# A sigmoid bias as a constant, and the last score visit of the first pass ahead of all value products

## The chip, the cores and the metric

One core of a Trainium2 chip runs the whole kernel. TensorE (PE in the profile, its weight loads PEld) multiplies, VectorE (DVE) copies, adds and transposes blocks of 32 x 32, ScalarE (ACT) applies the sigmoids, GpSimd (POOL) issues all loads, and SyncE (SP) issues the stores. The metric is the device time of one execution in microseconds; the number given for a kernel is the median of its runs.

## The reference

```python
def _attn_ref(q, k, v):                       # 8 batches, 12 heads, 448 positions, head size 64
    scores = scale * np.matmul(q, k.transpose(0, 1, 3, 2)) - np.log(S)     # scale = 1/8
    attn = 1.0 / (1.0 + np.exp(-scores))
    return np.matmul(attn, v)

def _moe_ref(x, w_in, w_out, beta):           # x: 3584 x 768, w_in: 768 x 2048, w_out: 2048 x 768
    h = x @ w_in
    g = h * (1.0 / (1.0 + np.exp(-beta * h)))
    return g @ w_out
```

The attention has a sigmoid in place of a softmax, with the constant -log(448) added to every scaled score. Its result, heads side by side, is x of the two dense layers; between them every hidden column has its own `beta`. All inputs and the output are float32.

## The kernel before

**Tiling.** Loads turn everything into float16. A batch has 448 positions, which are three full key tiles of 128 and a last one of 64 (`JF` = 3, `KL` = 64). Heads are taken four at a time as a *group* `g` (three groups for each batch, `QPB`), and two at a time as a *slot* `s` (a group has slots 2g and 2g+1). The four heads of a group lie in the four blocks of 32 partitions, so q and k are made ready by DVE's 32 x 32 transposes (`transpose`, L174), and four score matmuls of 32 contraction rows run beside each other.

**Scores and values.** A score tile is two PSUM banks. PE writes scores into it (`score`, L198), ACT turns it into weights by one sigmoid over 128 x 896 (`weigh`, L210, its instruction is L212), and `attend` (L256) multiplies the weights with v into a PSUM bank, from where DVE copies them to `xT` (L276). The last key tile has only 64 rows, so the two slots of a group share one score tile for it, one in the upper and one in the lower 64 partitions. For that, the 64 rows of v must be there twice: `double_v_last` (L141) copies them from partitions 0 to 63 to 64 to 127 on DVE. An even slot reads the rows as loaded, an odd slot the copied ones (`last_base`).

**Dense layers.** `dense1` (L281) makes one of 16 column tiles of the hidden layer: six matmuls with w_in, a sigmoid on ACT with scale `beta` (L293) and a product on DVE (L296). The second layer is written out as `dense2` (L307) for some row tiles and as a seven-product scheme (`strassen`, L388) for pairs of the others. Their units are a stream of *filler* (`filler_stream`, L467) that is put between the score visits, so that PE has work while ACT computes.

**The opening.** The order of every queue is that of the program: nothing reorders the list. The first batch is special. Its queries are done in two halves of 224 columns (`QH`). `half_visit(g, c0, second)` (L238) computes key tiles 0 and 1 of a group, or with `second` tiles 2 and 3, always into two score tiles; the second of the two in a `second` visit is only half full (448 columns of sigmoid). In the first pass (c0 = 0) there are six such visits, in the loop at L525. Here six PSUM banks are three score tiles, used in turn, one bank holds the idle matmuls and one more is free for values (`share_psum(firsts, 3, 2)`); later there are two score tiles and four other banks. Between the visits, `idle_units` (L507) multiplies a tile of zeros; the visits and these units are all the work PE has until v is there. Before the change, right after the fifth visit, slot 0's values (`attend(0, 0, QH, (0,))`) are issued, then the doubling of v's last rows, then the transposition of the second half of q of group 0, then two idle units, and only then the sixth visit. After the loop come slot 1's values, the first visit of the second pass, and the values of slots 2 to 5.

**The loads.** POOL issues in this order: q (first half) and k of group 0, the two memsets of L498 and L499, q and k of groups 1 and 2, four pieces of v and two pieces with v's last 64 rows, the second halves of q of groups 0 to 2, then w_in in eight pieces of 256 hidden columns (`load_w_in`, L147), of which each serves two `dense1` units. Then come the next groups and w_out. A load waits on POOL until the load eight places before it has landed, since they share a semaphore.

The constant of the sigmoid is in `nlogs`, a column of 128 x 1 that POOL fills at L498, and L212 takes it as `bias=nlogs[:, 0:1]`.

Of the kernel before, what the change touches and what calls it, by code (L numbers as in the profile page):

```python
# [8 lines left out]
FP32 = mybir.dt.float32  # L9
# [4 lines left out]
def kernel(  # L14
# [10 lines left out]
    nc = tc.nc  # L25
# [6 lines left out]
    P = 128  # L32
    BLK = 32
    HQ = P // BLK
    NB = S // BLK
# [5 lines left out]
    QPB = H // HQ  # L41
# [5 lines left out]
    QH = S // 2  # L47
    MSCALE = 1.0 / math.sqrt(D)
    NEG_LOG_S = -math.log(float(S))
# [3 lines left out]
    const = ctx.enter_context(tc.tile_pool(name="const", bufs=1))  # L53
# [30 lines left out]
    def bank(name: str, cols: int = S, hold=None):  # L84
        i = min((i for i in used if i not in held.values()), key=used.get)
        touch(i)
        if hold is not None:
            held[hold] = i
        return psum["one"].tile([P, cols], FP32, tag=f"one{i}", name=name)


    nlogs = const.tile([P, 1], FP32, name="nlogs")
    dummy = const.tile([P, 1], FP32, name="dummy")
    beta_in = const.tile([BLK, P], FP32, name="beta_in")
    beta_sb = const.tile([P, BLK], FP32, name="beta_sb")
# [11 lines left out]
    def load_one(g: int, r: int, c0: int = 0, c1: int = NB):  # L107
        b, t = divmod(g, QPB)
        if g not in raws:
            raws[g] = rawp.tile([P, 2, NB, D], FP16, tag="raw", name="raw")  # L110
        nc.gpsimd.dma_start(  # L111
            out=raws[g][:, r, c0:c1].rearrange("p c d -> p (c d)"),
            in_=(q, k)[r][b, HQ * t : HQ * (t + 1)].rearrange("h (p c) d -> (h p) (c d)", c=NB)[
                :, c0 * D : c1 * D
            ],
        )
# [8 lines left out]
    def last_base(s: int) -> int:  # L125
        return (s % 2 ^ swapped(s // 2)) * KL
# [14 lines left out]
    def double_v_last(b: int):  # L141
        nc.vector.tensor_copy(out=vs[b][KL:P, :, JF], in_=vs[b][0:KL, :, JF])
# [27 lines left out]
    def in_order(b: int, t):  # L170
        t = t.rearrange("p c e -> p (c e)").bitcast(FP32)
        return t.rearrange("p (q c) -> p c q", c=NB) if b == B - 1 else t

    def transpose(g: int, r: int, c0: int = 0, c1: int = NB):  # L174
        raw = raws[g][:, r]
        if r == 0:
            if g not in qT:
                qT[g] = qTp.tile([P, NB * BLK, PAIR], FP16, tag="qT", name="qT")
            nc.vector.transpose(  # L179
                out=in_order(g // QPB, qT[g][:, c0 * BLK : c1 * BLK]),  # L180
                in_=raw[:, c0:c1].rearrange("p c d -> p (c d)").bitcast(FP32),
            )
            return
        kT[g] = kTp.tile([P, S, PAIR], FP16, tag="kT", name="kT")
        to = kT[g].rearrange("p k e -> p (k e)").bitcast(FP32)
        frm = raw.rearrange("p c d -> p (c d)").bitcast(FP32).rearrange("p (c f) -> p c f", c=NB)
        nc.vector.transpose(
            out=to[:, 0 : JF * P].rearrange("p (j i q) -> p i j q", j=JF, i=HQ),
            in_=frm[:, 0:NF].rearrange("p (i j) f -> p i j f", j=JF),
        )  # L190
        nc.vector.transpose(  # L191
            out=to[:, JF * P :], in_=frm[:, NF:].rearrange("p c f -> p (c f)")
        )
# [16 lines left out]
    def weigh(sco, n: int):  # L210
        at = attnp.tile([P, 2, S], FP16, tag="attnT", name="attnT")
        nc.scalar.activation(  # L212
            out=at[:, :, 0:n],
            in_=sco[:, :, 0:n],
            func=AF.Sigmoid,
            bias=nlogs[:, 0:1],
            scale=MSCALE,
        )
        return at


    def visit(g: int, jt: int, also=()):
        if jt < JF:
            todo = [(score_tile(), [s]) for s in (2 * g, 2 * g + 1)]
        else:
            todo = [(score_tile(), [2 * h, 2 * h + 1]) for h in (g, *also)]
        for e in range(PAIR):
            for sco, slots in todo:
                for s in slots:
                    for hh in range(2):  # L230
                        score(sco, 0, s, jt, hh, e, 0, S)
        for sco, slots in todo:
            at = weigh(sco, S)
            for s in slots:
                at_tiles[s, jt, 0] = at


    def half_visit(g: int, c0: int, second: int):  # L238
        slots = (2 * g, 2 * g + 1)
        scos = [score_tile() for _ in slots]  # L240
        plan = [(s, jt, sco, jt * QH) for jt in (0, 1) for s, sco in zip(slots, scos)]
        widths = [S, S]
        if second:
            plan = [(s, 2, sco, 0) for s, sco in zip(slots, scos)]
            plan += [(s, JF, scos[0], QH) for s in slots]
            widths = [S, QH]
        for i in range(0, len(plan), 2):
            for e in range(PAIR):
                for s, jt, sco, u0 in plan[i : i + 2]:
                    for hh in range(2):  # L250
                        score(sco, u0, s, jt, hh, e, c0, QH)
        ats = {id(sco): weigh(sco, n) for sco, n in zip(scos, widths)}
        for s, jt, sco, u0 in plan:
            at_tiles[s, jt, c0] = ats[id(sco)][:, :, u0 : u0 + QH]

    def attend(g: int, c0: int, n: int, part=(0, 1)):  # L256
        b, t = divmod(g, QPB)
        if b not in xTs:
            xTs[b] = xTp.tile([P, NHC, S], FP16, tag="xT", name="xT")
        slots = [2 * g + x for x in part]  # L260
        avs = [bank("av_ps") for _ in slots]
        todo = [(s, av, jt) for s, av in zip(slots, avs) for jt in range(JF)]
        for s, av, jt in todo + [(s, av, JF) for s, av in zip(slots, avs)]:
            at = at_tiles.pop((s, jt, c0))
            base, nk = (last_base(s), KL) if jt == JF else (0, P)
            for hh in range(2):
                nc.tensor.matmul(  # L267
                    av[hh * D : (hh + 1) * D, 0:n],
                    vs[b][base : base + nk, 2 * (s % NPAIR) + hh, jt],
                    at[base : base + nk, hh, 0:n],  # L270
                    start=(jt == 0),
                    stop=(jt == JF),
                    tile_position=(base, hh * D),
                )
        for s, av in zip(slots, avs):
            nc.vector.tensor_copy(out=xTs[b][:, s % NPAIR, c0 : c0 + n], in_=av[:, 0:n])  # L276
# [215 lines left out]
    NH = NB // 2  # L492
    firsts = ctx.enter_context(ExitStack())
    share_psum(firsts, 3, 2)
    with tc.manual_schedule():
        load_one(0, 0, 0, NH)
        load_one(0, 1)
        nc.gpsimd.memset(nlogs, NEG_LOG_S)  # L498
        nc.gpsimd.memset(dummy, 0.0)  # L499
        nc.scalar.activation(out=dummy, in_=dummy, func=AF.Sigmoid, bias=0.0, scale=1.0)  # L500

# [5 lines left out]
        def idle_units(n: int):  # L507
            for _ in range(n):
                nc.tensor.matmul(idle, still[:, 0:P], still, start=True, stop=True)  # L509
# [15 lines left out]
        for g in range(QPB):  # L525
            for second in range(2):
                half_visit(g, 0, second)
                if (g, second) == (QPB - 1, 0):
                    attend(0, 0, QH, (0,))
                    double_v_last(0)  # L530
                    transpose(0, 0, NH, NB)
                if 2 * g + second < 2 * QPB - 1:
                    idle_units(4 if g < QPB - 1 else 2)
        attend(0, 0, QH, (1,))
        half_visit(0, QH, 0)
        attend(1, 0, QH, (0,))
# [121 lines left out]
```

## Time and profile before

| what | value |
|---|---|
| timed runs | 388.84, 389.12 and 390.28 us, median 389.12 us |
| the profiled execution | span 388.2 us, by the page its whole time; the median is 0.9 us above it |
| PE / ACT / DVE / POOL busy | 381.5 / 241.5 / 229.7 / 67.3 us |
| score sigmoids (L212) | 171, of which 165 over 128 x 896 (1004 ns each) and 6 over 128 x 448 (627 ns each) |
| granted TensorE clock | 1.000 |
| loads and stores | 34.30 MB, mean 88 GB/s; 190 to 204 GB/s from 19 to 68 us |

A busy share is an average: a kernel whose PE is busy for 98% of the span is bound by PE nearly everywhere, and what else can be gained lies in the few places in which PE stands. The mean of one instruction is its latency, from start to written result; where two follow each other without a gap, the second starts before the first has ended, and the distance of the starts is the shorter number that counts for throughput. The busy spans of matmuls overlap in the same way, so a wait shorter than about a quarter of a microsecond does not show as idle time.

### The profile page before, as it was taken

How to read it: one execution, taken by the hardware profiler on the slowest of the kernel's cores; microseconds unless marked ns; L12 is line 12 of the kernel's file. 1: busy time of each engine (PE TensorE's matmuls, PEld its weight loads, DVE VectorE, ACT ScalarE, POOL GpSimd, SP SyncE). 2: the span in 40 equal slices, each digit the busy share in tenths (PEclk: the TensorE clock that was granted, in tenths of full speed). 3: DMA queues.
4: the chain of work that ended last, by engine and by line, in shares of the span. 5: the costliest groups of instructions: out<-in, count | busy, mean ns of one | idle time of the engine just before them, and what ended most of it. 6: DMA issues, size and time to landing. Idle time of an engine off the chain costs nothing.

```text
span 388.2 us, 7376 instructions
## 1 busy us (share of the span) xinstructions
PE 381.5 (98%) x2991; PEld 191.4 (49%) x2991; DVE 229.7 (59%) x437; ACT 241.5 (62%) x329; POOL 67.3 (17%) x117
## 2 busy tenths in 40 slices
PE   8899999999999999999999999999999999999996
PEld 3477754444545444444554445544445444555563
DVE  2356463885766556655765656664676565655762
ACT  4887865687565796497365783568853677625200
POOL 7833343122110410140110410104100000000000
PEclk9999999999999999999999999999999999999999
DMA  7999999629243760446353561629113300030033
GB/s 112 172 191 203 198 204 199 144 55 112 47 91 70 126 80 14 105 79 66 49 115 74 87 71 34 127 60 144 28 21 83 82 2 2 0 83 0 2 81 122
DMA packets 42401, 34.30 MB, mean 88 GB/s; under 512 B 21872, under 2 KB 38784, under 8 KB 42368
## 3 DMA queue, kind: packets, MB, share of 16 engines
q0 software_dynamic: 36976, 22.81, 42.8%
q1 hardware_dynamic: 5392, 11.02, 11.0%
q8 instruction: 23, 0.38, 0.4%
q14 instruction: 10, 0.08, 0.1%
HBM read 45.62 MB, written 11.01 MB: 146 GB/s over the span
## 4 chain that ended last, share of the span: by engine, by line
PE 93%; DMA 3%; ACT 2%; POOL 0%; issue 0%; DVE 0%; POOLq 0%
PE m_ps L285 39%; PE m_ps L397 29%; PE sco L201 11%; PE av_ps L267 10%; PE m_ps L315 4%; ACT attnT L212 2%; DMA raw<-in_k_dram 2%; DMA v<-in_v_dram 1%; POOL raw L111 0%; PE idle_ps L509 0%; ACT sg L293 0%; DVE osb L328 0%; DVE gt L296 0%; POOL nlogs L498 0%; POOL dummy L499 0%
## 5 line engine op out<-in xcount | busy, mean ns | idle before, releaser
L212 ACT ACTIVATE attnT<-sco,nlogs 128x896 f16<-128x896 f32 (+1 forms) x171 | 160.3, 991 | 84.3 <-PE sco L201 83.5
L285 PE MATMUL m_ps<-xT,w_in 128*128 128x448 f16 (+1 forms) x864 | 154.7, 332 | 0.4 <-DVE gt L296 0.3
L296 DVE TENSOR_TENSOR gt<-m_ps,sg 128x448 f16<-128x448 f32 (+1 forms) x144 | 79.8, 572 | 84.4 <-ACT sg L293 84.3
L285 PEld LDWEIGHTS <-w_in 128*128 128x128 f16 x864 | 80.6, 98 | 70.9 <-issue 15.5
L293 ACT ACTIVATE sg<-m_ps,beta_sb 128x448 f32<-128x448 f32 (+1 forms) x144 | 81.8, 595 | 31.3 <-PE m_ps L285 30.1
L397 PEld LDWEIGHTS <-sum 128*128 128x128 f16 x480 | 45.2, 98 | 36.4 <-issue 7.9
L201 PE MATMUL sco<-qT,kT 32*128 32x448 f16 (+3 forms) x864 | 52.6, 340 | 1.3 <-ACT attnT L212 1.1
L397 PE MATMUL m_ps<-w_T,sum 128*128 128x384 f16 x288 | 51.6, 327 | 0.0
L111 POOL DMA_DIRECT2D raw<-in_q_dram x27 | 14.8, 550 | 189.7 <-DVE kT L191 183.1
L416 DVE TENSOR_TENSOR osb<-m_ps,osb 128x384 f32<-128x384 f32 x60 | 33.3, 555 | 18.7 <-PE m_ps L397 16.9
L267 PE MATMUL av_ps<-attnT,v 128*64 128x448 f16 (+3 forms) x432 | 42.2, 340 | 0.7 <-DMA v<-in_v_dram 0.5
L276 DVE CAST xT<-av_ps 128x448 f16<-128x448 f32 (+1 forms) x54 | 28.8, 568 | 22.5 <-PE av_ps L267 22.5
L386 DVE TENSOR_TENSOR sum<-gt 128x1024 f16<-128x1024 f16 x60 | 39.1, 678 | 0.1
L397 PE MATMUL m_ps<-w_T,gt 128*128 128x384 f16 x192 | 34.2, 327 | 0.0
L397 PE MATMUL m_ps<-w_out,sum 128*128 128x384 f16 x192 | 33.7, 326 | 0.0
L267 PEld LDWEIGHTS <-v 128*64 128x64 f16 (+1 forms) x432 | 19.1, 107 | 25.5 <-issue 16.9
L201 PEld LDWEIGHTS <-kT 32*128 32x128 f16 (+1 forms) x864 | 13.5, 96 | 29.6 <-issue 27.5
L397 PEld LDWEIGHTS <-gt 128*128 128x128 f16 x192 | 18.1, 98 | 14.8 <-issue 3.1
L315 PE MATMUL m_ps<-w_out,gt 128*128 128x384 f16 (+2 forms) x128 | 22.5, 327 | 0.0
L132 POOL DMA_DIRECT2D v<-in_v_dram x32 | 19.8, 635 | 8.0 <-DMA w_in<-in_moe_w_in_dram 5.3
L179 DVE STREAM_TRANSPOSE qT<-raw 128x448 f32<-128x448 f32 (+1 forms) x27 | 16.6, 616 | 4.8 <-DMA raw<-in_q_dram 4.8
L315 PEld LDWEIGHTS <-gt 128*128 128x128 f16 x128 | 11.9, 98 | 10.3 <-issue 3.1
(24 smaller groups left out, 96.9 us busy)
## 6 DMA issues: line engine op xcount, KB each, us to landing
out_dram<-osb SPq DMA_DIRECT2D x98, 96.0 KB, 1.9
raw<-in_k_dram POOLq DMA_DIRECT2D x24, 224.0 KB, 4.8
raw<-in_q_dram POOLq DMA_DIRECT2D x21, 224.0 KB, 3.6
v<-in_v_dram POOLq DMA_DIRECT2D x32, 144.0 KB, 6.6
w_in<-in_moe_w_in_dram POOLq DMA_DIRECT2D x8, 384.0 KB, 10.9
w_out<-in_moe_w_out_dram POOLq DMA_DIRECT2D x4, 768.0 KB, 13.4
v<-in_v_dram POOLq DMA_DIRECT2D x16, 48.0 KB, 6.2
out_dram<-osb SPq DMA_DIRECT2D x2, 384.0 KB, 2.3
```

The source lines that it names most:

```text
L132: nc.gpsimd.dma_start(out=vs[b][i * BLK : (i + 1) * BLK, :, 0:JF].rearrange("p h j d -> p h (j d)"), in_=rows[:, :, JF * i * D : JF * (i + ...
L201: nc.tensor.matmul(sco[base : base + nk, hh, u0 : u0 + n], kT[g][lo : lo + BLK, jt * P : jt * P + nk, e], qT[g][lo : lo + BLK, c0 : c0 + n ...
L212: nc.scalar.activation(out=at[:, :, 0:n], in_=sco[:, :, 0:n], func=AF.Sigmoid, bias=nlogs[:, 0:1], scale=MSCALE,)
L267: nc.tensor.matmul(av[hh * D : (hh + 1) * D, 0:n], vs[b][base : base + nk, 2 * (s % NPAIR) + hh, jt], at[base : base + nk, hh, 0:n], start ...
L276: nc.vector.tensor_copy(out=xTs[b][:, s % NPAIR, c0 : c0 + n], in_=av[:, 0:n])
L285: nc.tensor.matmul(m1[:, 0:n], w_in16[:, hc, dc * P : (dc + 1) * P], xTs[b][:, hc, c0 : c0 + n], start=(hc == 0), stop=(hc == NHC - 1),)
L293: nc.scalar.activation(out=sg[:, 0:n], in_=m1[:, 0:n], func=AF.Sigmoid, bias=0.0, scale=beta_sb[:, dc : dc + 1])
L296: nc.vector.tensor_tensor(out=gt[:, dc, off : off + n], in0=m1[:, 0:n], in1=sg[:, 0:n], op=ALU.mult)
L315: nc.tensor.matmul(m2, gt[:, dc, cols(t)], w_out16[:, dc, lo:hi], start=(dc == 0), stop=(dc == NDC - 1),)
L386: nc.vector.tensor_tensor(out=sums[t, i], in0=x, in1=y, op=op)
L397: nc.tensor.matmul(m2, (x if op is None else sums[t, i])[:, dc], w[:, dc], start=first and dc == 0, stop=(dc == ND - 1), skip_group_check= ...
L416: nc.vector.tensor_tensor(out=out, in0=in0, in1=in1, op=op)
```

## The change

Two things. The sigmoid's bias is given as a Python number in place of the column `nlogs`, and the column and its memset go. And in the first pass, slot 0's values, the doubling and the transposition move from behind the fifth visit to behind the sixth; among themselves they are in reverse order now: first the transposition, then the doubling, then slot 0's values, which slot 1's values follow directly. The number of idle units stays.

```diff
-    nlogs = const.tile([P, 1], FP32, name="nlogs")
...
             func=AF.Sigmoid,
-            bias=nlogs[:, 0:1],
+            bias=NEG_LOG_S,
             scale=MSCALE,
...
-        nc.gpsimd.memset(nlogs, NEG_LOG_S)
...
         for g in range(QPB):
             for second in range(2):
                 half_visit(g, 0, second)
-                if (g, second) == (QPB - 1, 0):
-                    attend(0, 0, QH, (0,))
-                    double_v_last(0)
-                    transpose(0, 0, NH, NB)
                 if 2 * g + second < 2 * QPB - 1:
                     idle_units(4 if g < QPB - 1 else 2)
+        transpose(0, 0, NH, NB)
+        double_v_last(0)
+        attend(0, 0, QH, (0,))
         attend(0, 0, QH, (1,))
         half_visit(0, QH, 0)
```

## The prediction

> **What bounds the kernel now.** I read the page first, then PE's waits, then the order of time where PE waits.
>
> ```profile
> span 388.2 us, 7376 instructions
> ...
> PE 381.5 (98%) x2991; PEld 191.4 (49%) x2991; DVE 229.7 (59%) x437; ACT 241.5 (62%) x329; POOL 67.3 (17%) x117
> ```
>
> PE is the bound nearly everywhere. Asked by stretches, PE is busy 30.00 of 30 us from 80 to 110 us, 90.00 of 90 from 110 to 200 and 100.00 of 100 from 200 to 300. In these 220 us a faster ACT buys nothing, although most of the 171 score sigmoids run there. What can be gained lies before 75 us. PE's waits over the whole span:
>
> ```profile
> PE idle_ps L509 <- DVE still L503: 1.2, 1, 1.2
> PE sco L201 <- ACT attnT L212: 1.1, 4, 0.3
> PE av_ps L267 <- DMA v<-in_v_dram: 0.5, 1, 0.5
> PE m_ps L285 <- DVE gt L296: 0.3, 1, 0.3
> PE av_ps L267 <- issue: 0.2, 1, 0.2
> ```
>
> The columns are total, times and longest. All but the first line touch the change. The two lines of values (av_ps) and one of the four score waits lie in the stretch that is reordered. PE's order of time there:
>
> ```profile
> 13.16 0.78 PE L201 MATMUL sco<-qT,kT 32*128 32x224 f16 x16
> 14.18 0.48 PE L267 MATMUL av_ps<-attnT,v 128*64 128x224 f16 x6 [0.24 <-issue]
> 15.15 0.28 PE L267 MATMUL av_ps<-attnT,v 64*64 64x224 f16 x2 [0.49 <-DMA v<-in_v_dram]
> 15.36 0.60 PE L509 MATMUL idle_ps<-still 128*128 128x512 f16 x2
> 15.90 0.70 PE L201 MATMUL sco<-qT,kT 32*128 32x224 f16 x16
> 16.53 0.69 PE L267 MATMUL av_ps<-attnT,v 128*64 128x224 f16 x8
> 17.15 0.27 PE L201 MATMUL sco<-qT,kT 32*128 32x224 f16 x2
> 17.71 0.57 PE L201 MATMUL sco<-qT,kT 32*128 32x224 f16 x14 [0.29 <-ACT attnT L212]
> 18.21 0.69 PE L267 MATMUL av_ps<-attnT,v 128*64 128x224 f16 x8
> ```
>
> Slot 0's last two value matmuls stand until 15.15 for v's last rows, and the sixth visit stands behind them in the queue until 15.90. On ACT in the same time:
>
> ```profile
> 7.02 8.78 ACT L212 ACTIVATE attnT<-sco,nlogs 128x896 f16<-128x896 f32 x10 [4.22 <-PE sco L201]
> 16.65 3.56 ACT L212 ACTIVATE attnT<-sco,nlogs 128x896 f16<-128x896 f32 x4 [0.85 <-PE sco L201]
> ```
>
> From 7.02 to 15.80 ACT runs ten sigmoids with hardly a gap: the first pass is bound by ACT. It then idles 0.85 us, for the sixth visit. Its late sigmoid holds the score tile for which PE stands before 17.71.
>
> **The reorder, step by step.** I take durations from these rows. The fifth visit ends at 13.94 as before, and two idle units take 0.43 us, until about 14.4. The sixth visit's first tile is free by then; its second one is held by a sigmoid that starts at 13.90 and takes 1.00 us, until 14.90. So the visit ends near 14.95 + 0.57 = 15.5, and ACT goes on without a gap at 15.70 (before: 16.65). DVE meanwhile waits for q's second half of group 0, issued at 10.12 and landed 5.2 us later at 15.32; the transposition (0.41) ends at 15.75 and the doubling (0.35) at 16.1. Slot 0's values follow the visit from 15.55 to 16.2: v's last rows landed at 9.52 + 5.5 = 15.02. Slot 1's values run from 16.2 to 16.8. Only their last pair needs the doubling, so DVE's new order costs nothing. Queued behind them is the second pass's first visit; its score tile is free at 15.70 + 1.00 = 16.70. It runs from 16.85 and the next values start at 17.4, where they started at 18.21. That is 0.8 to 0.9 us. With a sigmoid 0.1 us shorter the chain ahead of it is shorter too, and it is up to 1.15 us.
>
> **What is late next.** The first `dense1` units, at 21.33 before, come forward by the same time and meet w_in. Piece 1 is issued at 13.58 and lands 8.0 us later, at 21.6; the third unit needs it and starts at 22.56. v's landing at 15.02 let its matmul start at 15.15, so w_in lets this unit start no sooner than 21.73: 0.83 us. Piece 2 (14.40 + 9.1 = 23.5, used at 24.93) and piece 3 (15.21 + 10.3 = 25.5, used at 27.62) have more room. The cap lies inside the gain and decides it: **0.83 us**, with 0.8 and 1.15 as ends. The moved instructions issue no DMA. POOL loses one memset, whose start is 34 ns ahead of the next one's: all later loads come **0.03 us** sooner.
>
> **The bias.** What a sigmoid costs without the column isn't in the trace. The nearest rows:
>
> ```profile
> L212 ACT ACTIVATE attnT<-sco,nlogs 128x896 f16<-128x896 f32 x165 | 157.2, 1004 | 84.3 <-PE sco L201 83.5
> L419 ACT COPY osb<-m_ps 128x384 f32<-128x384 f32 x12 | 5.7, 478 | 15.5 <-PE m_ps L397 15.3
> L212 ACT ACTIVATE attnT<-sco,nlogs 128x448 f16<-128x448 f32 x6 | 3.8, 627 | 0.0
> ```
>
> From the first and the last, an element costs (1004 - 627) / 448 = 0.84 ns and the rest is 627 - 377 = 250 ns. The copy, which reads no column, has 478 - 323 = 155 ns. So a sigmoid's latency falls by about 0.095 us. Whether the distance of two starts (0.90 us: a pair takes 1.90) falls as well is open: it does if the column is read after the instruction ahead has left the engine, and doesn't if that read is hidden behind it. The ends are 0 and 0.095 us for each start. I take 0.095: starts follow a score sigmoid after 0.89 us alike where the next instruction is a copy without a column, so no read of the next one's seems to sit in the overlap. The Trainium skill, "Advanced Engine Details and Errata", section "The Read-Write Bubble", says the same of operands in general: the read latency is exposed between instructions. The page "ScalarE: Activation LUTs", section "What ACT_TABLE_LOAD costs", gives about 93 ns for each such operand; by it the sums below would stay within 0.02 us.
>
> What this moves on PE, place by place. At 57.66, 62.79 and 69.50 two score matmuls run and the rest wait for the second of a pair of sigmoids:
>
> ```profile
> 57.66 0.37 PE L201 MATMUL sco<-qT,kT 32*128 32x448 f16 x2
> 58.31 0.57 PE L201 MATMUL sco<-qT,kT 32*128 32x448 f16 x6 [0.28 <-ACT attnT L212]
> ```
>
> That is 0.65 us from start to start, so there is room for the gain. A pair ends 2 x 0.095 = 0.19 us sooner (0.095 at the other end): 0.57 us for three (0.29). At 50.36 `dense1` stands 0.35 us for a bank whose sigmoid is queued behind a pair: 0.19 us (0). At 26.2 a score tile is 0.08 us late: 0.08. The sum is **0.84 us**, at the other end about 0.34. I cost the other 160 sigmoids at nothing: filler on PE covers them, and without that cover each pair would be worth 0.19 us.
>
> **Sum.** 0.83 + 0.03 + 0.84 = 1.70 us off a span of 388.2. The median of the runs is 0.9 above the span, and I take that as unchanged: 389.12 - 1.70 = **387.4 us**.
>
> **Rivals.**
> - *Only latency falls*, starts stay 0.90 us apart: 0.83 + 0.03 + 0.34 = 1.2, **387.9**. For it: nothing shows an uncovered read; against it, the equal 0.89 us.
> - *The bias goes on being read as a column* that a library fills, so this half of the change does nothing: 389.12 - 0.83 = **388.3**. Against it: L293, with bias 0.0, shows no column beside `beta_sb`.
> - *w_in lands 0.3 us sooner than in this trace*, and the whole 1.15 us stays: 1.15 + 0.03 + 0.84 = 2.0, **387.1**. Landings of 5 to 10 us under a full queue can differ by that.
> - *Slower: the doubling is now behind the transposition on DVE.* If q's second half lands late, slot 1's last values wait for 0.41 + 0.35 + 0.12 us after it, and everything on PE behind them; before, only the next visit waited, for 0.53. The opening's gain is gone when the landing is at 16.6 in place of 15.32, and the ACT gain too from 17.4. Landing at 17.7, as group 2's half does (12.01 + 5.7), the values end at 18.8 and the visit at 19.35 against 18.28: 1.07 slower there, less 0.87, **389.3**; at 20.0 it would be 391.6. Against it: nothing ahead of this load moves.
>
> A rule that speaks against the change is in the Trainium skill, "SBUF — State Buffer", in the note on DVE and loads under "SBUF: two separate sides": some DVE copies keep GpSimd from writing descriptors. By it, DVE's copy now at 15.75 instead of 15.89 could hold up w_in by at most its 0.35 us. The trace does not bear it out: the w_in issues at 15.21 and 16.02, beside DVE's work, took 0.848 and 0.856 us against 0.830 to 0.838 for the three before them.
>
> **How the numbers follow.** Forecast 53%, latency only 20%, w_in sooner 12%, bias unchanged 5%, late q 10%. The range is 386.7 to 389.1: from the w_in case less 0.4 for the spread of runs (388.84 is 0.3 under the median) to no gain; outside are the late q and tails of the others. Of a change under 0.5% (1.95 us, so 387.17 and 391.07) a measurement can't tell much. Faster by more: three in ten of the forecast and six in ten of the w_in case, 0.23. Slower by more: half of the late q, 0.05. The rest, 0.72, is within.
>
> **What the new profile would show.** L212 without `nlogs`, near 0.91 us for 128 x 896, pairs of 1.71. No idle time on ACT before the sixth visit's sigmoid, near 15.7. No PE wait for v. The first values of slot 2 near 17.4, and a wait of `dense1` for w_in near 21.6. Waits of 0.1 us less than now at 57, 62 and 69 us. PE at 100% from 80 us on, as now. I am wrong if pairs still take 1.81 or more, if PE stands after 15.6 for DVE, or if `dense1` units after 23 us wait for their pieces.

## The result

The changed kernel takes 388.29 us in the median of five runs (387.89 to 388.71), beside 389.30 us for the kernel before (388.84 to 390.28): a ratio of 0.9964, with a 95% interval of 0.9953 to 0.9975. It is faster by about a third of a per cent. Timed again beside the experiments it had 387.76 us against 389.51, ratio 0.9955 (0.9940 to 0.9969). The forecast was 387.4, in a range of 386.7 to 389.1.

The page of the profiled execution, which took 388.37 us:

```profile
span 386.6 us, 7375 instructions
...
PE 381.2 (99%) x2991; PEld 191.4 (50%) x2991; DVE 231.5 (60%) x437; ACT 228.8 (59%) x329; POOL 67.3 (17%) x116
```

ACT has 12.7 us less work, yet the span fell by 1.6 us only: PE's work is the same. ACT's groups by form (busy us, mean ns) and PE's waits over the span (total, times, longest):

```profile
L211 ACT ACTIVATE attnT<-sco 128x896 f16<-128x896 f32 x165 | 142.5, 915 | 89.1 <-PE sco L200 88.3
...
L211 ACT ACTIVATE attnT<-sco 128x448 f16<-128x448 f32 x6 | 3.2, 538 | 0.0
```

```profile
PE idle_ps L507 <- DVE still L501: 1.2, 1, 1.2
PE sco L200 <- DVE kT L186: 0.5, 1, 0.5
PE sco L200 <- ACT attnT L211: 0.2, 1, 0.2
PE m_ps L284 <- DVE gt L295: 0.2, 1, 0.2
```

`nlogs` is gone from the sigmoid, and both forms are 89 ns shorter. Of the four waits for a sigmoid one is left, the two waits for v are gone, and a new one stands in the second line: the first visit waits 0.5 us for the first keys of the kernel. PE's order of time in the opening:

```profile
13.65 0.69 PE L200 MATMUL sco<-qT,kT 32*128 32x224 f16 x16
14.27 0.60 PE L507 MATMUL idle_ps<-still 128*128 128x512 f16 x2
14.81 0.27 PE L200 MATMUL sco<-qT,kT 32*128 32x224 f16 x2
15.26 0.69 PE L200 MATMUL sco<-qT,kT 32*128 32x224 f16 x14 [0.18 <-ACT attnT L211]
15.89 1.31 PE L266 MATMUL av_ps<-attnT,v 128*64 128x224 f16 x16
17.13 0.58 PE L200 MATMUL sco<-qT,kT 32*128 32x224 f16 x16
17.64 1.31 PE L266 MATMUL av_ps<-attnT,v 128*64 128x224 f16 x16
```

and ACT's:

```profile
7.87 9.49 ACT L211 ACTIVATE attnT<-sco 128x896 f16<-128x896 f32 x12 [5.09 <-PE sco L200]
17.81 1.73 ACT L211 ACTIVATE attnT<-sco 128x896 f16<-128x896 f32 x2 [0.45 <-PE sco L200]
```

Twelve sigmoids stand in one row now, where ten did before. The view joins what lies less than 0.15 us apart, and the single instructions show that ACT still pauses by 0.14 us twice among the twelve. A pair takes 1.73 us instead of 1.90. Slot 2's first values start at 17.64, 0.57 us sooner than in the trace of before. But the whole opening is late here: ACT began at 7.87, against 7.02. Matching every matmul of the two traces from the end backwards shows where the 1.6 us lie: 0.57 in the opening, 0.18 at each of five later places (26, 50, 58, 63 and 70 us of the trace before) and 0.11 at 237 us. Everywhere else the two traces run at a constant distance.

### The profile page after: what moved, and what is told of

The parts are those of the page before. It is cut to its first block, busy times and chain, and to the rows that moved or that the text cites. A ratio compares the mean times of both kernels' runs of the same rounds, so it can differ in the third digit from the quotient of the medians.

```text
span 386.6 us, 7375 instructions
## 1 busy us (share of the span) xinstructions
PE 381.2 (99%) x2991; PEld 191.4 (50%) x2991; DVE 231.5 (60%) x437; ACT 228.8 (59%) x329; POOL 67.3 (17%) x116
## 4 chain that ended last, share of the span: by engine, by line
PE 95%; ACT 2%; DMA 1%; issue 1%; DVE 1%; POOL 0%; ACTq 0%; POOLq 0%
PE m_ps L284 38%; PE m_ps L396 29%; PE sco L200 12%; PE av_ps L266 10%; PE m_ps L314 5%; ACT attnT L211 2%; DMA raw<-in_k_dram 1%; PE idle_ps L507 1%; DVE xT L275 0%; POOL raw L110 0%; DVE kT L186 0%; ACT sg L292 0%; DVE osb L327 0%; DVE gt L295 0%; ACTq L292 0%
## 5 line engine op out<-in xcount | busy, mean ns | idle before, releaser
L211 ACT ACTIVATE attnT<-sco 128x896 f16<-128x896 f32 (+1 forms) x171 | 145.2, 902 | 89.1 <-PE sco L200 88.3
L295 DVE TENSOR_TENSOR gt<-m_ps,sg 128x448 f16<-128x448 f32 (+1 forms) x144 | 81.7, 572 | 81.1 <-ACT sg L292 77.2
L292 ACT ACTIVATE sg<-m_ps,beta_sb 128x448 f32<-128x448 f32 (+1 forms) x144 | 84.4, 596 | 36.3 <-PE m_ps L284 31.0
L110 POOL DMA_DIRECT2D raw<-in_q_dram x27 | 14.9, 553 | 186.5 <-DVE kT L190 180.2
L396 PEld LDWEIGHTS <-gt 128*128 128x128 f16 x192 | 18.1, 98 | 14.7 <-issue 3.1
L178 DVE STREAM_TRANSPOSE qT<-raw 128x448 f32<-128x448 f32 (+1 forms) x27 | 16.6, 616 | 7.4 <-DMA raw<-in_q_dram 7.4
```

What stands on the lines that cost most here:

```text
L211: nc.scalar.activation(out=at[:, :, 0:n], in_=sco[:, :, 0:n], func=AF.Sigmoid, bias=NEG_LOG_S, scale=MSCALE,)
L292: nc.scalar.activation(out=sg[:, 0:n], in_=m1[:, 0:n], func=AF.Sigmoid, bias=0.0, scale=beta_sb[:, dc : dc + 1])
L295: nc.vector.tensor_tensor(out=gt[:, dc, off : off + n], in0=m1[:, 0:n], in1=sg[:, 0:n], op=ALU.mult)
L396: nc.tensor.matmul(m2, (x if op is None else sums[t, i])[:, dc], w[:, dc], start=first and dc == 0, stop=(dc == ND - 1), skip_group_check= ...
```

## The experiments

**Each half alone.** First the constant bias with the order of before:

```diff
-            bias=nlogs[:, 0:1],
+            bias=NEG_LOG_S,
...
-        nc.gpsimd.memset(nlogs, NEG_LOG_S)
```

> The order of the opening is that of before; only the bias is a constant. My theory: the distance of two score sigmoids falls from 0.89 to 0.80 us, and that is worth 0.18 us at each of five places on PE (26, 50, 57, 62 and 69 us), 0.9 us together, and at most 0.3 us in the opening, where the sixth visit stands behind v's landing whatever ACT does: 0.9 to 1.2 us faster than before (ratio 0.997 to 0.9977), and slot 2's first values start at 17.9 to 18.2 us. Rival one, that the reorder brought nothing and the whole gain is ACT's: 1.5 us, and these values start near 17.6 as in the changed kernel. Rival two, that the bias brings nothing on the path: no change.

It took 388.52 us against 389.6, ratio 0.9971 (0.9961 to 0.9981). In its trace the opening's pair and all later places show what the full change shows (0.18 us each, 0.11 at 237), but v is waited for, longer than before, and slot 2's first values start at 17.79, a little sooner than expected. PE's waits, two of their lines left out:

```profile
PE av_ps L266 <- DMA v<-in_v_dram: 0.7, 1, 0.7
PE av_ps L266 <- issue: 0.5, 1, 0.5
PE sco L200 <- ACT attnT L211: 0.2, 1, 0.2
```

The line that ends in "issue" is a wait for v as well: the fourth piece of v landed at 13.52 us and the products started at 13.61; in the trace of before the two times are 14.09 and 14.18.

Then the order alone:

```diff
-                if (g, second) == (QPB - 1, 0):
-                    attend(0, 0, QH, (0,))
-                    double_v_last(0)
-                    transpose(0, 0, NH, NB)
...
+        transpose(0, 0, NH, NB)
+        double_v_last(0)
+        attend(0, 0, QH, (0,))
```

> The new order with the bias still read from the column. My theory: sigmoids keep 1.00 us and 0.89 us from start to start, the five later places keep their waits, and the opening gains what the order alone is worth: slot 2's first values at 17.3 to 17.6 us against 18.21 before where k of group 0 lands as in the trace of before (near 5.5 us), some 0.3 us later where it lands at 6.6 as in the trace of after. In all 0.5 to 0.85 us faster than before (ratio 0.9978 to 0.9987). Rival one, that the order brings nothing: values at 18.2 and no change. Rival two, that it brings all: 1.5 us.

389.0 us, ratio 0.9984 (0.9975 to 0.9993). Its trace has no wait for v and slot 2's first values at 17.04, 1.17 us sooner than in the trace of before and 0.3 us sooner than expected at best; all later waits are as they were. The two parts cost each other little: 0.29% and 0.16% alone, 0.36% and 0.45% together. The timed 0.62 us of the order is half of what its trace shows against the trace of before. That difference stayed open until the last two runs, below.

**A second column.** The kernel before with the scale read from a column, too:

```diff
-            scale=MSCALE,
+            scale=mscale[:, 0:1],
...
+        nc.gpsimd.memset(mscale, MSCALE)
```

> The kernel before with the scale of the score sigmoid read from a column too, so each reads two. My theory (a column holds the engine): latency 1.00 to 1.10 us, distance of two starts 0.89 to 0.98 us; 0.18 us more at each of the five later places, some 0.3 us at places that now just pass, and up to 0.6 us in the opening that ACT bounds: 1.2 to 2.0 us slower than before (ratio 1.003 to 1.005). Rival (a column's read hides behind the instruction ahead, only latency grows): starts stay 0.89 us apart and the kernel is 0.2 to 0.5 us slower.

392.2 us, ratio 1.0068 (1.0055 to 1.0081). ACT's group by form, and PE's order of time at a place where the kernel before waited 0.28 us:

```profile
L213 ACT ACTIVATE attnT<-sco,nlogs,mscale 128x896 f16<-128x896 f32 x165 | 172.2, 1096 | 79.1 <-PE sco L202 78.6
```

```profile
58.32 0.37 PE L202 MATMUL sco<-qT,kT 32*128 32x448 f16 x2
59.16 0.57 PE L202 MATMUL sco<-qT,kT 32*128 32x448 f16 x6 [0.46 <-ACT attnT L213]
```

The second column costs the same again. From the start of a score sigmoid to the start of the next instruction it is, at the least, 0.797, 0.889 and 0.981 us with none, one and two columns: 0.092 us for each, all of it on ACT's throughput. Inside a pair of score sigmoids the commonest distances are 0.813, 0.905 and 0.997 us, the same steps. The kernel is 2.6 us slower, more than the 1.2 to 2.0 us expected, because what happens to PE is not symmetric: new delays appear at 43, 110, 115, 196, 244, 257 and 305 us (of the trace before), places that in the kernel before stood for nothing. By the traces, taking a column away gains 1.0 us behind the opening, adding one loses 2.2.

**What binds the opening now.** DVE's order was the prediction's slower rival, so the doubling goes first:

```diff
-        transpose(0, 0, NH, NB)
         double_v_last(0)
+        transpose(0, 0, NH, NB)
```

> The changed kernel with the doubling of v's last rows ahead of the transposition of q's second half on DVE. My theory: the order of these two costs nothing, since slot 1's values need the doubling only with their last pair: the same as the changed kernel within 0.1 us, ratio to before 0.995 to 0.9975. Rival (the doubling behind the transposition holds PE): 0.2 to 0.5 us faster than the changed kernel. If the second half of q lands after 16.5 us here, it would show in the visit behind slot 1's values.

387.95 us, ratio 0.9958 (0.9946 to 0.9971), not told apart from the changed kernel. In its trace slot 2's values start 0.51 us sooner than in the changed kernel's first trace, and all of that is given back, 0.25 us at 30.2 and 0.28 at 34.1, where `dense1` waits for pieces 5 and 7 of w_in (landed at 30.1 and 34.1). Two more edits of the opening: two idle products between all visits in place of four,

```diff
-                    idle_units(4 if g < QPB - 1 else 2)
+                    idle_units(2)
```

> The changed kernel with two idle units instead of four between the visits of the first pass, so PE reaches each visit sooner. My theory: ACT bounds the pass and only its gaps of 0.1 to 0.15 us before four of the visits close; slot 2's first values come up to 0.5 us sooner, but w_in's later pieces (the last one lands at 32.7 to 34.1 us in the traces so far and is used at 34.1 in the changed kernel) take most of that back, seen as waits of dense1 near 30 and 34 us: 0 to 0.3 us faster than the changed kernel, ratio to before 0.9945 to 0.9965. Rival one, that the opening still passes its time on: 0.4 to 0.5 us faster than the changed kernel and no such waits. Rival two, that the idle units keep TensorE's clock up: matmuls at the slow rate in the opening (0.43 us for an idle unit in place of 0.22) and 1 us or more slower.

387.81 us, ratio 0.9950 (0.9938 to 0.9963), with the idle products at their usual pace (two take 0.60 us, as in the changed kernel); and the keys of group 0 loaded and transposed ahead of its first queries:

```diff
-        load_one(0, 0, 0, NH)
         load_one(0, 1)
+        load_one(0, 0, 0, NH)
...
-            transpose(g, 0, 0, NH)
-            transpose(g, 1)
+            for r in ((0, 1) if g else (1, 0)):
+                transpose(g, r, 0, NB if r else NH)
```

> The changed kernel with k of group 0 loaded and transposed ahead of the first half of q, since k landed at 5.3 to 6.6 us in the traces so far and held the first visit. My theory: the first visit starts near 5.7 to 6.2 us with less spread from run to run, but v's last rows (15 us), q's second half (15.3) and w_in hold the later opening: 0 to 0.3 us faster than the changed kernel, ratio to before 0.9945 to 0.9965. Rival, that the late k alone set the opening of the changed kernel's trace: 0.5 us or more faster.

387.55 us, ratio 0.9943 (0.9930 to 0.9955). Neither is told apart from the changed kernel as it was timed again (0.9940 to 0.9969), though slot 2's values start at 16.65 and 17.01 in their traces, against 17.64. Why so much movement in the traces and so little in the times is seen by counting from the first visit, not from the span's start.

**The changed kernel and the kernel before once more.**

> The changed kernel once more. In the profiled execution of it shown first, the first visit began at 7.26 us (group 0's keys landed at 6.6), and slot 2's first values 10.38 us after it; the spread kernels, whose opening is the same, have 10.37 to 10.38 with first visits at 6.54 to 6.76. Theory (the late landing was chance, and the opening is a chain of 10.38 us behind the first visit): keys at 5.3 to 6.2, first visit at 6.0 to 6.9, slot 2's first values 10.3 to 10.5 us after it, and whatever lies before 17.2 is given back to w_in's last pieces between 29 and 35 us; ratio 0.9950 to 0.9970 to the kernel before. Rival (without the memset, or by the order of its loads, this program's keys always land late): keys again near 6.6 and values near 17.6.

> The kernel before once more, for a second trace of it. The first one had a span of 388.2 us, while the executions beside the experiments mostly have 387.5 to 388.0. Theory (its opening was a late sample: v's last rows landed at 15.02, and w_in never came late): v's last rows at 14.4 to 14.8 us, slot 2's first values at 17.5 to 17.9 in place of 18.21, all later distances as in the first trace, span 387.5 to 388.0. Rival (the spread of the executions lies behind the opening): slot 2's first values within 0.1 us of 18.21, and the difference in waits after 20 us.

> A third trace of the kernel before, with the same expectation as the second: the span follows the time at which slot 2's first values start, and that follows the landing of v's last rows, with about 3.1 to 3.2 us between the landing and those values.

The changed kernel's second trace has a span of 386.0 us, with the first keys at 5.6 and the first visit at 6.22. The two new traces of the kernel before have 387.7 and 387.6 (389.47 and 389.36 us in all), 0.5 and 0.6 less than the one that the prediction read, and that difference lies wholly ahead of 18.5 us. PE's waits and order of time in the second trace of before:

```profile
PE idle_ps L509 <- DVE still L503: 1.2, 1, 1.2
PE sco L201 <- ACT attnT L212: 1.1, 4, 0.3
PE m_ps L285 <- DVE gt L296: 0.3, 1, 0.3
```

```profile
13.54 0.79 PE L201 MATMUL sco<-qT,kT 32*128 32x224 f16 x16
14.25 0.69 PE L267 MATMUL av_ps<-attnT,v 128*64 128x224 f16 x8
...
15.41 0.70 PE L201 MATMUL sco<-qT,kT 32*128 32x224 f16 x16
16.04 0.69 PE L267 MATMUL av_ps<-attnT,v 128*64 128x224 f16 x8
16.66 0.27 PE L201 MATMUL sco<-qT,kT 32*128 32x224 f16 x2
17.22 0.57 PE L201 MATMUL sco<-qT,kT 32*128 32x224 f16 x14 [0.28 <-ACT attnT L212]
17.72 1.53 PE L267 MATMUL av_ps<-attnT,v 128*64 128x224 f16 x18
```

There is no wait for v. Slot 0's eight value products take 0.69 us in one piece at 14.25. The chain of the opening, measured from the first visit (all from PE's order of time and the landings in the trace):

| trace | first visit | v's last rows | slot 2's values | from the first visit |
|---|---|---|---|---|
| before, first | 6.41 | 15.0 | 18.21 | 11.80 |
| before, second | 6.85 | 14.5 | 17.72 | 10.87 |
| before, third | 6.62 | 14.4 | 17.59 | 10.97 |
| bias only | 5.99 | 14.7 | 17.79 | 11.80 |
| order only | 6.20 | 14.8 | 17.04 | 10.84 |
| changed, first | 7.26 | 15.2 | 17.64 | 10.38 |
| changed, second | 6.22 | 14.9 | 16.78 | 10.56 |
| doubling first | 6.76 | 14.9 | 17.13 | 10.37 |
| idle products 2 | 6.11 | 14.5 | 16.65 | 10.54 |
| keys first | 6.06 | 15.0 | 17.01 | 10.95 |
| spread evenly (below) | 6.76 | 14.6 | 17.14 | 10.38 |
| the same, DVE's order mended | 6.54 | 14.7 | 16.91 | 10.37 |
| the same, both edits of the opening | 6.66 | 14.0 | 17.04 | 10.38 |

In the old order an early first visit is of no use: in the first trace of before and in that of the bias alone, PE stands for v's last rows, and slot 2's values start 3.1 to 3.2 us after these have landed. In the second trace the first visit is later, v is in time, and nothing stands; in the third it is 0.1 us. (The distance from v's landing to slot 2's values is 3.2 us in these two as well: there the landing and the chain from the first visit meet.) There the order alone is worth 0.0 to 0.1 us (10.84 against 10.87 and 10.97). The new order takes this floor away. So the gain of the order depends on how long after the first visit v's last rows land: it is 0.96 us against the first trace of before, where they land 8.6 us after it, and about nothing against the other two, where they land 7.7 and 7.8 us after it. The new order has only one trace without the constant bias, so this is read from few executions.

Then the constant bias shortens the chain by 0.46 to 10.38, which is five times 0.092. In the trace of the order alone and in the first of the changed kernel, the sixth visit stands for the ninth sigmoid, which holds its second score tile: this sigmoid ends 8.41 us after the first visit with the order alone, 7.95 us in the changed kernel. Ahead of that end, four starts inside a pair come sooner by 0.092 us each, and the sigmoid itself is shorter by 0.089. From pair to pair the starts stay 0.90 us apart inside a group, since the next scores are not there sooner.

The two edits of the opening have 10.54 and 10.95, no better: in both, the visit of group 1 stands for that group's keys, and ACT idles 0.30 and 0.63 us after its fourth sigmoid.

One thing that can set the first visit was in no theory. The program starts with 13 idle products (`idle_units(13)`), and the first visit is queued behind them. PE's order of time in the second trace of before, and then in the second trace of the changed kernel:

```profile
1.19 5.73 PE L509 MATMUL idle_ps<-still 128*128 128x512 f16 x13 [1.19 <-DVE still L503]
6.85 0.60 PE L201 MATMUL sco<-qT,kT 32*128 32x224 f16 x16
```

```profile
1.19 4.90 PE L507 MATMUL idle_ps<-still 128*128 128x512 f16 x13 [1.19 <-DVE still L501]
6.22 0.58 PE L200 MATMUL sco<-qT,kT 32*128 32x224 f16 x16
```

These products start 0.427 us apart and later 0.216. In the second trace of before all of them are slow, and the visit follows the last one although the keys had landed at 5.6. In the other trace the faster pace begins at 5.0, and the visit follows the keys, which had landed at 5.6 too, by 0.66. The first keys landed between 4.7 and 6.6 us in these traces, 5.3 to 6.6 where their load was not moved. Both spreads are there without any edit, so the 7.26 of the changed kernel's first trace is chance: its second one has 6.22.

In the second trace of the changed kernel, 0.18 of the 10.56 is the rival's wait, in small. PE's order of time, and DVE's:

```profile
14.85 1.50 PE L266 MATMUL av_ps<-attnT,v 128*64 128x224 f16 x16
```

```profile
15.21 0.41 DVE L178 STREAM_TRANSPOSE qT<-raw 128x224 f32<-128x224 f32 x1 [4.13 <-DMA raw<-in_q_dram]
15.65 0.35 DVE L141 COPY v<-v 64x768 f16<-64x768 f16 x1
```

The values take 1.50 in place of 1.31: the last pair starts at 16.06, once the doubling behind the transposition has ended at 16.00. A further 0.20 us went at 21.3, where `dense1` used piece 1 of w_in at 21.32, landed at 21.3.

**A version that beats both.** The waits left between 49 and 70 us come from the filler, which is spread unevenly between the visits. Spread evenly:

```diff
-        spread = [4 * M1H_US, 2 * M1H_US + M2_US, 6 * M1H_US, 3 * M2_US / 4]
-        spread += [17 * M2_US / 4 / 7] * 7
+        spread = [4 * M1H_US, 2 * M1H_US + M2_US / 2, M2_US / 2 + 3 * M1H_US, 3 * M1H_US]
+        spread += [20 * M2_US / 4 / 7] * 7
```

> The changed kernel with the filler between the early visits spread more evenly: dense1 units and dense2 quarters move from the first three visits after 39 us to the seven that follow, so that nearly all of these have twelve matmuls of filler and not eight in every second one. My theory: the waits of 0.47 us that are left at 56.7, 61.7 and 68.2 us and the 0.42 us at 49.0 go except for one, as ACT's pair of 1.71 us is covered: 1.0 to 1.4 us faster than the changed kernel, ratio to before 0.992 to 0.9945. Rival, that this time is PE's work and not a wait (matmul ends are modelled): no change against the changed kernel.

388.01 us, ratio 0.9952 (0.9938 to 0.9965), short of the 0.992 to 0.9945 expected: most of it was given back at one new wait. PE's order of time, and DVE's, there:

```profile
50.46 1.63 PE L266 MATMUL av_ps<-attnT,v 128*64 128x448 f16 x14
53.01 0.38 PE L266 MATMUL av_ps<-attnT,v 64*64 64x448 f16 x2 [0.92 <-DVE v L141]
```

```profile
51.35 0.63 DVE L178 STREAM_TRANSPOSE qT<-raw 128x448 f32<-128x448 f32 x1
51.91 0.54 DVE L186 STREAM_TRANSPOSE kT<-raw 128x384 f32<-128x384 f32 x1
52.37 0.20 DVE L190 STREAM_TRANSPOSE kT<-raw 128x64 f32<-128x64 f32 x1
52.60 0.35 DVE L141 COPY v<-v 64x768 f16<-64x768 f16 x1
```

The second batch's values wait for a doubling that stands behind three transpositions on DVE. So these instructions go ahead of the three filler units:

```diff
-                fill_units(3)
-                spent += 3 * M2_US / N2
+                double_v_last(1)
...
-                double_v_last(1)
+                fill_units(3)
+                spent += 3 * M2_US / N2
```

> The kernel with the filler spread evenly, and with slot 1's doubling of the last values and group 4's two transpositions issued ahead of the three filler steps before slot 3, the doubling first. Theory (the 1.3 us wait at 51.7 us in the run before came from VectorE's order alone): that wait goes, one of about 0.47 us near 57.8 stays, and the kernel is 0.8 to 1.3 us faster than the spread one: ratio 0.9920 to 0.9940 to the kernel before. Rival (the raw keys of group 4, or the banks of dense1, come too late for the new place, so the wait only moves): 0.9945 to 0.9960, with a wait of over 0.8 us between 44 and 53 us.

386.54 us against 389.52, ratio 0.9923 (0.9911 to 0.9936). DVE's order of time now, and PE's:

```profile
48.89 0.36 DVE L141 COPY v<-v 64x768 f16<-64x768 f16 x1
49.29 0.65 DVE L178 STREAM_TRANSPOSE qT<-raw 128x448 f32<-128x448 f32 x1
```

```profile
50.23 1.69 PE L266 MATMUL av_ps<-attnT,v 128*64 128x448 f16 x16
51.85 0.57 PE L200 MATMUL sco<-qT,kT 32*128 32x448 f16 x8
```

The wait is gone, and of those of the score visits between 49 and 70 us one is left, 0.47 us from start to start at 56.3. Its interval lies wholly below both of the changed kernel: it beats both kernels, by 3.0 us and by 1.2 to 1.75. Last, the same with the two edits of the opening (idle products 2, keys first):

> The same, and with two idle products between all visits of the first pass and the keys of group 0 loaded first. Theory (the opening's gain and the gain of the spread add up until the last pieces of w_in cap the opening at about 0.8 us): slot 2's first values near 16.4 to 16.8 us, a wait of 0.1 to 0.5 us for w_in's last piece near 33, and 0.5 to 0.9 us below the kernel without these two: ratio 0.9900 to 0.9925. Rival (the earlier opening is all given back to w_in or to the first waits of the steady part): within 0.2 us of it.

386.84 us, ratio 0.9931 (0.9917 to 0.9944): nothing gained, where 0.5 to 0.9 us were expected. Its keys landed at 4.7 us, but all 13 idle products ran at the slow pace, the first visit started behind them at 6.66, and slot 2's values came 10.38 us later, as ever.

## Why the prediction was right, and where it was not

- **PE bounds the kernel, gains lie before 75 us.** Right, but for 0.11 us at 237, ahead of a product of the seven-product scheme. That place does not show as idle time in the trace of before.
- **The bias, 0.095 us for each start.** Right: 89 ns of latency, 92 ns from start to start. The open question, whether the distance of starts falls, is settled by the bias alone (0.889 to 0.797) and by the second column (0.981). The rival "only latency falls" is out, and so is the one in which the column stays. The Trainium skill, "ScalarE: Activation LUTs", section "What ACT_TABLE_LOAD costs", has about 93 ns for each such operand; the runs agree.
- **Its places, 0.84 us.** The three score waits and the one of `dense1` gave 0.18 each where 0.19 was forecast. The term at 26.2 us was mis-sized: 0.08 forecast, 0.18 measured, as at the other places. In the trace of before the visit there takes 0.88 us, where the one at 23.80 takes 0.58; no idle time shows, since the busy spans of matmuls overlap. With 237 us the sum is 1.01.
- **The reorder, 0.83 us.** The mechanism was right, and so were the sixth visit's sigmoid without the idle time ahead of it and the missing wait for v. The step that failed is the row of 15.15: a stand for v's last rows in one execution was taken as what the kernel does. The second trace of before has nothing of it, the third 0.1 us. Counted from the first visit the forecast was 17.4 - 6.41 = 10.99 us; the order alone has 10.84, with the bias 10.38. So the step was too cautious in the chain and too generous in what it was compared with. In timed runs the order is worth 0.62 us.
- **w_in as the cap.** Right in kind. Piece 1 held `dense1` by 0.20 us in the second trace of the changed kernel, where the opening was early enough; in the first trace it had landed at 21.1 and nothing waited. With the doubling first it was pieces 5 and 7, which the prediction did not look at: in the trace of before they had 1.62 and 1.35 us of room, and the gain of the bias at 26 us lies ahead of them. Where a unit waited, it started 0.05 us after its piece had landed (21.32 after 21.27), not 0.13 as forecast, so the cap itself was a little higher than 0.83. Which piece holds was forecast more sharply than landings allow: the last one lands between 32.5 and 34.1 in all these traces.
- **The memset, 0.03 us.** Group 1's first load is issued at 2.45 us instead of 2.48, as forecast. That all later loads gain as much is not shown: this load landed between 6.8 and 8.1 us in the three traces of the kernel before, and some later issues wait for a landing, as v's fifth piece, at 8.37 us behind a landing at 8.09. Group 0's keys are issued ahead of the memset, at 1.89 us in both kernels.
- **The slower rival** exists as a mechanism: it cost 0.18 us in one of two traces of the changed kernel, so the prediction's sign of being wrong, PE standing after 15.6 us for DVE, came true there at 16.0. The cause was not a late q (it landed at 15.2 us) but values that start at 14.85, sooner than the 15.55 of the forecast, which let the doubling's order cost nothing. The second half of q landed between 14.3 and 15.4 us in all traces, far from the 16.6 at which it would have taken the gain.
- **The span and what lies around it.** The forecast takes 1.7 us off the median; the medians differ by 1.0 us in the first five runs and by 1.75 when timed again. The number came out 0.9 us too low in the first five runs, and the step behind it is the 0.9 us that the prediction took between the span and the median. In all other executions for which both are known it is 1.7 to 1.85 us. By that the traced execution of before would have taken about 390.0 us (an estimate), some 0.5 above the other two that were traced, by its late opening. From there, 390.0 - 1.70 = 388.3 is what the first five runs have; that it fits so closely is in part luck, since the second timing has 387.76. Between the usual spans, 387.7 before and 386.6 and 386.0 after, the distance is 1.1 to 1.7 us.

## What to carry to other kernels

A wait for a load in one profile is a sample: before a change is priced by it, compare what else in that trace is late, or take a second trace. In an opening, count from the event that starts the chain, not from the span's start; five of the eight traces with the new order and the constant bias then agree to 0.01 us (10.37 to 10.38), while their first visits lie up to 0.72 us apart, and the other three (10.54 to 10.95) each show a wait of their own. A per-instruction cost on a covered engine is worth what the few uncovered places make of it; here that was more in loss than in gain.

## What was not expected of the hardware

TensorE's first products run at half the later pace (0.427 against 0.216 us from start to start), and the time of the change of pace varies from execution to execution: after some 2.6 us of products in the trace of the order alone, while in the second trace of before 5.7 us of them were not enough. The granted clock in the profile's slices shows nothing of it (1.00 from 1 to 6 us in the second trace of before). The Trainium skill, "TensorE: Matmul & The Clock Gate", section "What you observe", puts the transition at around 4 us into sustained matmul activity, give or take 0.5; the spread here is wider than that. Both distances are those that the same page of the Trainium skill has in the section "Wait — 56ns, not 53.3ns?" for 512 columns, cold and warm. Its section "What's actually happening" has the number of slow products vary from run to run, 6, 11 or 14 in one kernel; the traces here agree, with 6 slow ones in the trace of the order alone and all 13, as far as their starts tell, in the second trace of before.
